# w2's first 352 rows on eight DMA engines instead of 224 on five, in a decode kernel of attention and a gated feed-forward

## The chip, the cores and the metric

The kernel runs on one core of a Trainium2 chip. Its time is the device time of one execution in microseconds; several executions are timed and the median is given. A profile belongs to one further execution, with its own time: there, "span" is the time from the first instruction's start to the last one's end on the core.

## What is computed

Two sequences, one new token each (B = 2), model width 512, 32 heads of 128, a cache of 4096 keys and values a head, all in bfloat16. An attention output and a small feed-forward output are mixed by a gate that each sequence computes from its own token:

```python
def _A_ref(x, k_cache, v_cache, wq, wo):
    q = (x @ wq)                                        # (2, 32, 1, 128)
    scores = jnp.einsum("bhqd,bhkd->bhqk", q, k) * (Dh ** -0.5)
    p = _softmax(scores, axis=-1)
    o = jnp.einsum("bhqk,bhkd->bhqd", p, v)
    return o.reshape(B, Sq, Hq * Dh) @ wo               # wo: 4096 x 512

def _B_ref(x, w1, w2):
    h = jnp.maximum(x @ w1, 0)                          # w1: 512 x 1376
    return h @ w2                                       # w2: 1376 x 512

g = _sigmoid((x * gate_w).sum(-1, keepdims=True))
return g * _A_ref(x, ...) + (1 - g) * _B_ref(x, ...)
```

The two caches are 134 MB of the 145 MB that are read. There is little arithmetic for each byte, so the kernel is a stream of loads with work fitted in between.

## The kernel before, in words

**Program order.** Every instruction is written down once for its engine by `P.add`, with the names of the events it waits for (`waits`), DMA semaphores with counts (`dwaits`) and the event it signals. `emit` (L67) writes these lists out, one for each of SP, TensorE (pe), VectorE (dve), ScalarE (act) and GpSimd (pool). An engine runs its own list in order; across engines only the events count.

**The load stream.** All large loads are issued by SP, in one list (L215 to L242). First w1 and wq, then sixteen units of 8 MB: eight of the K cache and eight of the V cache, in the order k0 to k4, v0, k5, v1, k6, v2, k7, v3 to v7. The units go round three regions of `kv`, 64 KB a partition each (`NREG`, `REG`); a unit's load waits until the unit three places earlier has been consumed (`freed`). The last V unit comes in two pieces, v7a (192 of 256 rows a partition) and v7b (64). Behind them, in the region of the fourteenth unit (v5), come the weights of the output stage, all issued when v5 has been consumed: w2p (L231 and L234), wo in three pieces wo0, wo1, wo2 (L236: 16, 12 and 4 rows a partition), and w2a, w2b, w2c, w2d (L239). The last SP issue is the store of the result (L242), which waits for both casts.

A load over 128 partitions moves eight rows on each of the sixteen DMA engines, and each engine works through its own rows of SP's list in order.

**How w2 is laid out.** w2 has 1376 rows of 512 numbers, 1 KB each. `W2` (L210) lists pieces as (semaphore, first row, rows a partition, first block). Before the change 1152 rows, nine blocks of 128, go over all 128 partitions: w2a and w2b with three consecutive rows a partition, w2c with two, w2d with one. The first 224 rows go over few partitions: 220 of them as eleven consecutive rows on 20 partitions, by four transfers of five partitions each (`j::4`, L231), 11 KB a partition, and four rows as one block on four partitions (L234). Together 21 blocks (`NF`).

**The feed-forward half.** `ffn_h` (L306) runs early: for each block four matmuls (L312) over w1 columns spaced by the block's rows a partition, so that h comes out with row i of a block on the partition where w2's row lies; then ScalarE writes relu(h) x (1 - g) into `hT` (L318), once for each sequence and each group of blocks with the same number of partitions.

**The end.** `v_unit` (L423) multiplies probabilities by V; `v_extract`, `v_gather` and `o_scale` bring the attention output together, `o_place` spreads it over the partitions as `oW`. The output stage adds matmuls of one block each, two halves of 256 columns (`step`, L475), into one accumulator: `project_first` (L479) the w2p blocks, of which five stand ahead of v7's gather and the others behind it, waiting for all five w2p transfers (count 80); then `project` (L485) the 32 blocks of wo and, in order, those of w2a, w2b, w2c and w2d, each group waiting for its own transfer. The block with `stop` lets VectorE and ScalarE cast the two halves (L496, L498), and SP stores 2 KB.

**TensorE's code.** TensorE has some 2180 of the program's 2394 recorded instructions; beside the loads, the DMA queue "instruction" (q8) brings 16 KB pieces of code while the kernel runs.

Of the kernel before, what the change touches and what calls it, by code (L numbers as in the profile page):

```python
# [84 lines left out]
def bass_gated_mix__gqa_block_cached__dense_activation_relu__decode_kernel(  # L85
# [16 lines left out]
    kv = sb("kv", [128, NREG, REG], bf16)  # L102
# [26 lines left out]
    hT = sb("hT", [128, 21, 2], bf16)  # L129
# [24 lines left out]
    def psf(p0, p1, c0, n):  # L154
        return PSF[p0:p1, c0:c0 + n]

    for e in ("pe", "dve", "act", "pool"):
        P.sems[e] = nc.alloc_semaphore(e + "_ev")
    names = ["x", "gw", "wq", "w1", "v7a", "v7b", "w2p", "wo0", "wo1", "wo2", "w2a", "w2b", "w2c", "w2d", "cast", "out"]
    sem = {n: nc.alloc_semaphore("sem_" + n) for n in names}  # L160
    sem_reg = [nc.alloc_semaphore(f"sem_reg{s}") for s in range(NREG)]

# [13 lines left out]
    def freed(what):  # L176
        kind, u = what
        return f"pe_sc_{u}" if kind == "k" else f"pe_v_{u}"

    def sp(fn, waits=(), dwaits=()):  # L180
        P.add("sp", fn, waits=waits, dwaits=dwaits)
# [4 lines left out]
    def dve(fn, waits=(), signal=None, dwaits=()):  # L186
        P.add("dve", fn, waits=waits, signal=signal, dwaits=dwaits)

    def act(fn, waits=(), signal=None, dwaits=()):
        P.add("act", fn, waits=waits, signal=signal, dwaits=dwaits)  # L190

    def pe(fn, waits=(), signal=None, dwaits=()):
        P.add("pe", fn, waits=waits, signal=signal, dwaits=dwaits)
# [10 lines left out]
    wo_reg = place[("v", 7)] + 1  # L204
    WO = wo_reg % NREG
    wo_sb = kv[:, WO, 0:16384]
    w2_sb = kv[:, WO, 16384:27136].rearrange("p (r n) -> p r n", n=512)


    W2 = (("w2p", 0, 11, 0), ("w2p", 220, 1, 11), ("w2a", 224, 3, 12), ("w2b", 608, 3, 15), ("w2c", 992, 2, 18), ("w2d", 1248, 1, 20))  # L210
    NF = 21

    act(lambda e: e.dma_start(x_sb[0:2], A_x.rearrange("b s d -> (b s) d")).then_inc(sem["x"], 16))
    act(lambda e: e.dma_start(x_sb[2:3], gate_w.rearrange("(o d) -> o d", o=1)).then_inc(sem["gw"], 16))
# [2 lines left out]
    for n, what in enumerate(order):  # L217
        if n >= NREG:
            waits = [freed(order[n - NREG])]
        else:  # L220
            waits = ["pe_h", "dve_setup", "act_q"] if n == C else []
# [5 lines left out]
        else:  # L227
            sp(lambda e, n=n, what=what: e.dma_start(kv[:, n % NREG, :], unit_in(what)).then_inc(sem_reg[n % NREG], 16),
               waits=waits)
    for j in range(4):  # L230
        sp(lambda e, j=j: e.dma_start(w2_sb[j:20:4, 0:11, :].rearrange("p r n -> p (r n)"),  # L231
                                      B_w2[0:220, :].rearrange("(p r) n -> p (r n)", r=11)[j::4]).then_inc(sem["w2p"], 16),
           waits=([freed(order[wo_reg - NREG])] if j == 0 else []))
    sp(lambda e: e.dma_start(w2_sb[0:4, 11, :], B_w2[220:224, :]).then_inc(sem["w2p"], 16))  # L234
    for i, (a, b) in enumerate(((0, 16), (16, 28), (28, 32))):
        sp(lambda e, i=i, a=a, b=b: e.dma_start(wo_sb[:, a * 512:b * 512], A_wo.rearrange("(p r) n -> p (r n)", r=32)[:, a * 512:b * 512])  # L236
           .then_inc(sem[f"wo{i}"], 16))
    for name, row, n, r0 in W2[2:]:
        sp(lambda e, name=name, row=row, n=n, r0=r0: e.dma_start(  # L239
            w2_sb[:, r0:r0 + n, :].rearrange("p r n -> p (r n)"),  # L240
            B_w2[row:row + 128 * n, :].rearrange("(p r) n -> p (r n)", p=128)).then_inc(sem[name], 16))
# [64 lines left out]
    def ffn_h():  # L306
        for ft in range(NF):
            row, n, r0 = [(row, n, r0) for _, row, n, r0 in W2 if r0 <= ft < r0 + n][0]
            m = 20 if ft < 11 else 4 if ft == 11 else 128
            for t in range(4):  # L310
                o = t * DFF + row + ft - r0
                pe(lambda e, ft=ft, t=t, o=o, n=n, m=m: e.matmul(psf(0, m, H_C0 + 2 * ft, 2), lhsT=w1_sb[:, o:o + (m - 1) * n + 1:n],  # L312
                                                            rhs=xT32[:, t, 0:2], start=(t == 0), stop=(t == 3)),
                   dwaits=([(sem["w1"], 16)] if ft == 0 and t == 0 else []),
                   signal=("pe_h" if ft == NF - 1 and t == 3 else None))
        for b in range(2):
            for p, r0, r1 in ((20, 0, 11), (4, 11, 12), (128, 12, NF)):
                act(lambda a, b=b, p=p, r0=r0, r1=r1: a.activation(  # L318
                    out=hT[0:p, r0:r1, b], in_=psf(0, p, H_C0 + 2 * r0, 2 * (r1 - r0))[:, b::2], func=ACT.Relu, scale=gm[0:p, b:b + 1]),
                    waits=(["pe_h", "act_gm"] if b + r0 == 0 else []), signal=(f"act_h{b}" if r1 == NF else None))  # L320

# [134 lines left out]
    def o_scale(b):  # L456
        dve(lambda v: v.tensor_reduce(out=Osum[:], in_=psf(0, 32, O_C0, 512).rearrange("p (c d) -> p d c", c=4), axis=AX.X, op=ALU.add),
            waits=[f"pe_g_{4 * b + 3}"], signal=f"dve_S{b}")
        dve(lambda v: v.tensor_scalar(out=O_sb[:, b, :], in0=Osum[:], scalar1=rinv[:, b:b + 1],
                                      scalar2=gb[0:32, b:b + 1], op0=ALU.mult, op1=ALU.mult),  # L460
            waits=[f"dve_S{b}"], signal=f"dve_O{b}")
# [11 lines left out]
    def step(w, m, start=False, stop=False, waits=[], dwaits=[]):  # L473
        for g in range(2):
            pe(lambda e, g=g: e.matmul(psf(64 * g, 64 * g + 2, FIN_C0, 256), lhsT=w, rhs=m[:, 256 * g:256 * g + 256],  # L475
                                       start=start, stop=stop, tile_position=(0, 64 * g), skip_group_check=True),
               waits=(waits if g == 0 else []), dwaits=(dwaits if g == 0 else []), signal=("pe_fin" if stop and g else None))

    def project_first(r0, r1):  # L479
        for r in range(r0, r1):  # L480
            k = 20 if r < 11 else 4
            step(hT[0:k, r, :], w2_sb[0:k, r, :], start=(r == 0), waits=(["act_h1", "act_exp1"] if r == 0 else []),
                 dwaits=([(sem["w2p"], 80)] if r == 0 else []))

    def project():  # L485
        lands = {0: "wo0", 16: "wo1", 28: "wo2"}
        for r in range(32):
            step(oW[:, r, :], wo_sb[:, r * 512:r * 512 + 512], waits=(["act_oW"] if r == 0 else []),
                 dwaits=([(sem[lands[r]], 16)] if r in lands else []))
        for name, _, n, r0 in W2[2:]:  # L490
            for r in range(r0, r0 + n):
                step(hT[:, r, :], w2_sb[:, r, :], stop=(r == NF - 1), dwaits=([(sem[name], 16)] if r == r0 else []))
        for g in range(2):
            src, dst = psf(64 * g, 64 * g + 2, FIN_C0, 256), out_sb[:, 256 * g:256 * g + 256]
            if g == 0:
                dve(lambda e, src=src, dst=dst: e.tensor_copy(out=dst, in_=src).then_inc(sem["cast"], 1), waits=["pe_fin"])  # L496
            else:
                act(lambda e, src=src, dst=dst: e.activation(out=dst, in_=src, func=ACT.Copy).then_inc(sem["cast"], 1), waits=["pe_fin"])  # L498
# [5 lines left out]
    w_block(0)  # L504
    w_block(1)
    ffn_h()
    for u in range(4):
        k_turn(u)
# [10 lines left out]
    for v in range(8):  # L519
        v_unit(v)  # L520
        if v == 3:
            o_denominator()
        v_extract(v)
        if v < 3:
            spread(v + 1)
            k_turn(5 + v)
            k_scores(5 + v)
            if v == 0:
                w_block(7)
        if v == 2:  # L530
            sm_max(1)
            sm_exp(1)
            sm_turn(1)
        if v == 7:
            project_first(0, 5)
        v_gather(v)
        if 3 <= v < 7:
            spread(v + 1)
        if v == 3:
            o_scale(0)  # L540
    project_first(5, 12)
    o_scale(1)
    o_place()
    project()
    tail_sp[0]()

# [31 lines left out]
```

## Time and profile before

| | |
|---|---|
| median of 3 runs | 343.61 us (343.56 to 343.7) |
| the profiled execution: its time, its span | 343.64 us, 342.3 us |
| bytes read | 145.43 MB, 425 GB/s over the span |
| TensorE / VectorE busy | 189.9 us / 155.2 us |
| w2p issued (first of four) | at 294.73 us |
| last block's matmuls begin | at 340.35 us |
| cast, store issued | 340.67 us, 341.11 us |

Each core has sixteen DMA engines; "DMA share" in a stretch is the mean busy share of the sixteen. The chain of waits follows the work that ended last back to what released it. A row of the timeline gives the start, the duration, the engine and line, the operation, the tile written and those read, and in brackets how long the engine had been idle and what ended that. "hT" as source marks w2's blocks, "oW" those of wo.

### The profile page before, as it was taken

To read this page: it belongs to the slowest core of one execution; us is meant where nothing else is said; L and a number is where in the kernel's file an instruction comes from. 1 tells how busy PE (TensorE), PEld (TensorE's weight loads), DVE (VectorE), ACT (ScalarE), POOL (GpSimd) and SP (SyncE) were. 2 spreads that over 40 slices of the span, in tenths; PEclk is the share of its full clock that TensorE was granted. 3 is DMA by queue.
4 is the path that set the end of the run, shared out by engine and by line. 5 is a ranking of instruction groups with operands and counts; after the bars stand their busy time and mean duration, and the time that the engine had idled before them with its cause. 6 is when DMAs were issued, how large, how long until landed. Compare 5 with 4: busy or idle time off the path is not lost.

```text
span 342.3 us, 2394 instructions
## 1 busy us (share of the span) xinstructions
PE 189.9 (55%) x1282; PEld 39.4 (12%) x898; DVE 155.2 (45%) x41; ACT 13.1 (4%) x31; POOL 43.1 (13%) x55
## 2 busy tenths in 40 slices
PE   0160069795968909850993059800994522506385
PEld 0040001010100101010011001200111201102132
DVE  1010797979899769219900694009925000000010
ACT  2010000000000020000000000000003000000000
POOL 2000000000000004042005000050003150413200
PEclk9995559899896967995799559965898585858589
DMA  8998989899998989899999999899999999999996
GB/s 349 429 484 375 483 375 483 383 475 414 438 490 368 490 383 475 383 469 391 467 406 446 429 429 483 375 484 406 452 406 452 406 446 421 437 440 427 389 422 253
DMA packets 3810, 145.56 MB, mean 425 GB/s; under 512 B 445, under 2 KB 582, under 8 KB 1094
## 3 DMA queue, kind: packets, MB, share of 16 engines
q1 hardware_dynamic: 3796, 145.43, 98.6%
q8 instruction: 8, 0.13, 0.2%
q10 hardware_dynamic: 6, 0.00, 0.0%
HBM read 145.43 MB, written 0.00 MB: 425 GB/s over the span
## 4 chain that ended last, share of the span: by engine, by line
DMA 64%; PE 23%; DVE 10%; SPq 2%; issue 0%
DMA kv<-in_A_k_cache_dram 43%; PE PS L340 14%; DMA kv<-in_B_w_dram 11%; DVE kv L335 10%; DMA kv<-in_A_v_cache_dram 10%; PE PS L368 5%; PE PS L423 3%; SPq L231 1%; SPq L239 0%; SPq L236 0%; PE PS L475 0%; PE PS L443 0%; SPq L234 0%; DVE ptm L496 0%; SPq L216 0%
## 5 line engine op out<-in xcount | busy, mean ns | idle before, releaser
L335 DVE STREAM_TRANSPOSE kv<-kv 128x8192 uint32<-128x8192 uint32 x16 | 138.5, 8690 | 80.3 <-DMA kv<-in_A_k_cache_dram 80.3
L340 PE MATMUL PS<-kv,zero 128*128 128x512 bf16 x384 | 117.5, 417 | 0.0
L368 PE MATMUL PS<-kv,zero 128*128 128x512 bf16 x128 | 54.1, 423 | 89.6 <-DVE kv L335 81.5
L423 PE MATMUL PS<-kv,ptm 128*32 128x512 bf16 x512 | 40.0, 459 | 33.8 <-DMA kv<-in_A_v_cache_dram 33.8
L368 PEld LDWEIGHTS PS<-kv,zero 128*128 128x128 bf16 x128 | 13.3, 104 | 203.6 <-issue 112.3
L406 POOL TENSOR_TENSOR ptm<-E,mask 128x512 bf16<-128x512 bf16 x32 | 32.2, 1039 | 10.9 <-DVE E L397 10.0
L434 DVE TENSOR_TENSOR X<-PS,maskc 128x512 f32<-128x512 f32 x1 | 0.7, 691 | 63.7 <-PE PS L423 63.7
L423 PEld LDWEIGHTS PS<-kv,ptm 128*32 128x32 bf16 x512 | 16.4, 112 | 58.4 <-issue 49.7
L438 POOL TENSOR_TENSOR X<-X,maskc 128x512 f32<-128x512 f32 x7 | 7.3, 1038 | 112.6 <-ACT X L437 112.6
L328 POOL TENSOR_TENSOR zero<-q_sb,mask 128x32 bf16<-128x32 bf16 x8 | 1.9, 251 | 151.2 <-PE PS L340 132.4
L443 PE MATMUL PS<-X,zero 128*32 128x512 f32 x16 | 8.5, 614 | 6.8 <-POOL X L438 6.6
L437 ACT ACTIVATE X<-PS 128x512 f32<-128x512 f32 x7 | 4.2, 596 | 142.4 <-PE PS L423 142.4
L292 PE MATMUL PS<-kv,zero 128*32 128x512 bf16 x32 | 3.6, 628 | 8.9 <-DMA kv<-in_A_wq_dram 8.9
L374 DVE TENSOR_REDUCE zero<-PS 128x2 f32<-128x2048 f32 x2 | 4.5, 2272 | 7.2 <-PE PS L340 7.2
L397 DVE STREAM_TRANSPOSE E<-E 128x2048 bf16<-128x2048 bf16 x2 | 4.6, 2311 | 4.7 <-ACT E L389 4.7
L299 DVE STREAM_TRANSPOSE ptm<-PS 128x1024 f32<-128x1024 f32 x1 | 1.2, 1249 | 11.9 <-PE PS L292 11.9
L381 ACT ACTIVATE nrow<-mmax 128x32 f32<-128x32 f32 x2 | 0.5, 228 | 138.0 <-DVE mmax L378 138.0
L475 PE MATMUL PS<-kv,oW 128*2 128x256 bf16 x64 | 3.8, 272 | 2.4 <-DMA kv<-in_A_wo_dram 2.4
L496 DVE CAST ptm<-PS 2x256 bf16<-2x256 f32 x1 | 0.4, 412 | 9.1 <-PE PS L475 9.1
L389 ACT ACTIVATE E<-PS,negm 128x1024 bf16<-128x1024 f32 x4 | 4.4, 1109 | 0.6 <-DVE negm L385 0.6
L270 PE MATMUL PS<-kv 3*128 3x3 bf16 x4 | 0.3, 167 | 6.5 <-DMA kv<-in_gate_w_dram 6.5
L475 PE MATMUL PS<-kv,hT 20*2 20x256 bf16 (+2 forms) x42 | 3.2, 269 | 0.9 <-DMA kv<-in_B_w_dram 0.8
(43 smaller groups left out, 26.5 us busy)
## 6 DMA issues: line engine op xcount, KB each, us to landing
kv<-in_A_v_cache_dram SPq DMA_DIRECT2D x1, 6144.0 KB, 47.5
kv<-in_A_wq_dram SPq DMA_DIRECT2D x1, 4096.0 KB, 14.9
kv<-in_A_v_cache_dram SPq DMA_DIRECT2D x1, 2048.0 KB, 52.0
kv<-in_A_wo_dram SPq DMA_DIRECT2D x1, 2048.0 KB, 34.3
kv<-in_A_wo_dram SPq DMA_DIRECT2D x1, 1536.0 KB, 37.6
kv<-in_B_w_dram SPq DMA_DIRECT2D x1, 1376.0 KB, 5.8
kv<-in_B_w_dram SPq DMA_DIRECT2D x2, 384.0 KB, 39.1
kv<-in_A_wo_dram SPq DMA_DIRECT2D x1, 512.0 KB, 38.4
```

What stands on the lines that cost most here:

```text
L335: dve(lambda v, h=h: v.transpose(out=reg[:, 8192 * h:8192 * (h + 1)], in_=reg[:, 8192 * h:8192 * (h + 1)]), dwaits=([landed(what)] if h == ...
L340: return e.add_instruction(mybir.InstMatmult(name=nc.get_next_instruction_name(), engine=mybir.EngineType.PE, ins=[e.lower_ap(rhs), e.lowe ...
L368: return e.matmul(dst, lhsT=w, rhs=m, start=first, stop=final, skip_group_check=True)
L374: dve(lambda v: v.tensor_reduce(out=mpad[:, 0:2], in_=PSF[:, 0:2048].rearrange("p (x h q) -> p h x q", h=2, q=16), axis=AX.XY, op=ALU.max) ...
L389: act(lambda a, h=h: a.activation(out=E[:].rearrange("p (x h q) -> p h x q", h=2, q=16)[:, h], in_=PSF[:, 0:2048].rearrange("p (x h q) -> ...
L397: dve(lambda v: v.transpose(out=E[:], in_=E[:]), waits=[f"act_exp{b}"], signal=f"dve_et{b}")
L406: pool(lambda g, src=src, dst=dst: g.tensor_tensor(out=dst, in0=src, in1=msk, op=ALU.mult), waits=(([f"dve_et{b}"] if ub == 0 else []) + ( ...
L423: pe(lambda e, ci=ci, t=t: e.matmul(psf(32 * t, 32 * t + 32, c0, 512), lhsT=ptm[:, ci].rearrange("p c h -> p (c h)"), rhs=rows[:, 512 * ci ...
L437: act(lambda e: e.activation(out=X2[:], in_=src, func=ACT.Copy), waits=[f"pe_v_{v}"], signal=f"act_x_{v}")
L438: pool(lambda e: e.tensor_tensor(out=X, in0=X, in1=msk, op=ALU.mult), waits=[f"act_x_{v}"] + ([] if v else ["dve_setup"]), signal=f"pool_x ...
L443: pe(lambda e: e.matmul(psf(0, 32, O_C0, 512), lhsT=selx[:, 24 - 8 * ub:56 - 8 * ub], rhs=X2[:], start=(ub == 0), stop=(ub == 3), skip_gro ...
L475: pe(lambda e, g=g: e.matmul(psf(64 * g, 64 * g + 2, FIN_C0, 256), lhsT=w, rhs=m[:, 256 * g:256 * g + 256], start=start, stop=stop, tile_p ...
```

## The change

The first 352 rows of w2 take the place of the 224: 32 partitions with eleven consecutive rows each, by four transfers of eight partitions; the transfer of four rows is gone. The other 1024 rows are eight blocks over 128 partitions, in transfers of five, two and one rows a partition instead of three, three, two and one. The blocks become 19, and the matmuls of `ffn_h`, the relu's groups and the steps of the output stage follow.

```diff
-    W2 = (("w2p", 0, 11, 0), ("w2p", 220, 1, 11), ("w2a", 224, 3, 12), ("w2b", 608, 3, 15), ("w2c", 992, 2, 18), ("w2d", 1248, 1, 20))
-    NF = 21
+    W2 = (("w2p", 0, 11, 0), ("w2a", 352, 5, 11), ("w2b", 992, 2, 16), ("w2c", 1248, 1, 18))
+    NF = 19
...
     for j in range(4):
-        sp(lambda e, j=j: e.dma_start(w2_sb[j:20:4, 0:11, :].rearrange("p r n -> p (r n)"),
-                                      B_w2[0:220, :].rearrange("(p r) n -> p (r n)", r=11)[j::4]).then_inc(sem["w2p"], 16),
+        sp(lambda e, j=j: e.dma_start(w2_sb[j:32:4, 0:11, :].rearrange("p r n -> p (r n)"),
+                                      B_w2[0:352, :].rearrange("(p r) n -> p (r n)", r=11)[j::4]).then_inc(sem["w2p"], 16),
            waits=([freed(order[wo_reg - NREG])] if j == 0 else []))
-    sp(lambda e: e.dma_start(w2_sb[0:4, 11, :], B_w2[220:224, :]).then_inc(sem["w2p"], 16))
...
-    for name, row, n, r0 in W2[2:]:
+    for name, row, n, r0 in W2[1:]:
...
-            m = 20 if ft < 11 else 4 if ft == 11 else 128
+            m = 32 if ft < 11 else 128
...
-            for p, r0, r1 in ((20, 0, 11), (4, 11, 12), (128, 12, NF)):
+            for p, r0, r1 in ((32, 0, 11), (128, 11, NF)):
...
-            k = 20 if r < 11 else 4
-            step(hT[0:k, r, :], w2_sb[0:k, r, :], start=(r == 0), waits=(["act_h1", "act_exp1"] if r == 0 else []),
-                 dwaits=([(sem["w2p"], 80)] if r == 0 else []))
+            step(hT[0:32, r, :], w2_sb[0:32, r, :], start=(r == 0), waits=(["act_h1", "act_exp1"] if r == 0 else []),
+                 dwaits=([(sem["w2p"], 64)] if r == 0 else []))
...
-    project_first(5, 12)
+    project_first(5, 11)
```

## The prediction

> **What bounds the kernel now.** I read the chain of waits first.
>
> ```profile
> DMA 64%; PE 23%; DVE 10%; SPq 2%; issue 0%
> DMA kv<-in_A_k_cache_dram 43%; PE PS L340 14%; DMA kv<-in_B_w_dram 11%; DVE kv L335 10%; DMA kv<-in_A_v_cache_dram 10%; PE PS L368 5%; PE PS L423 3%; SPq L231 1%; SPq L239 0%; SPq L236 0%; PE PS L475 0%; PE PS L443 0%; SPq L234 0%; DVE ptm L496 0%; SPq L216 0%
> ...
> q1 hardware_dynamic: 3796, 145.43, 98.6%
> q8 instruction: 8, 0.13, 0.2%
> ```
>
> The loads keep the sixteen DMA engines busy for 98.6% of the span, so TensorE's and VectorE's shares are work inside that stream: the end comes when the last weight bytes land. How the stream ends is in the timeline and in the table by stretches (us; PE, PEld, DVE, ACT, POOL; clock; DMA share; GB/s).
>
> ```profile
> 338.49 0.20 PEld L475 LDWEIGHTS PS<-kv,hT 128*2 128x2 bf16 x6 [0.65 <-DMA kv<-in_B_w_dram]
> ...
> 340.07 0.09 PEld L475 LDWEIGHTS PS<-kv,hT 128*2 128x2 bf16 x4 [0.43 <-DMA kv<-in_B_w_dram]
> 340.35 0.08 PEld L475 LDWEIGHTS PS<-kv,hT 128*2 128x2 bf16 x2 [0.20 <-DMA kv<-in_B_w_dram]
> ...
> 340.67 0.41 DVE L496 CAST ptm<-PS 2x256 bf16<-2x256 f32 x1 [9.05 <-PE PS L475]
> 341.11 0.27 SPq L242 DMA_DIRECT2D out_dram<-ptm  x1
> ```
>
> ```profile
> 337.00:337.50 0.50, 0.50 (x14) 0.34 (x8) 0.00 (x0) 0.00 (x0) 0.00 (x0) 1.00 1.01 389
> 337.50:338.00 0.50, 0.50 (x12) 0.28 (x8) 0.00 (x0) 0.00 (x0) 0.00 (x0) 1.00 0.99 377
> 338.00:338.50 0.50, 0.15 (x6) 0.01 (x2) 0.00 (x0) 0.00 (x0) 0.00 (x0) 1.00 0.82 322
> 338.50:339.00 0.50, 0.49 (x6) 0.17 (x6) 0.00 (x0) 0.00 (x0) 0.00 (x0) 1.00 0.84 322
> 339.00:339.50 0.50, 0.06 (x2) 0.07 (x4) 0.00 (x0) 0.00 (x0) 0.00 (x0) 1.00 0.70 252
> ```
>
> TensorE waits for w2a to w2d as each lands. From 338.0 the DMA share is 0.82 to 0.84: about three of sixteen engines have nothing left while the others carry on for 1.5 us.
>
> Which three? The trace holds every packet's start, duration and size, but no engine number. On one engine a packet starts within some 5 ns of the end of the one before, so packets can be strung into sixteen chains (span time: stamp less 11.40 us, the first instruction's). Near ties can swap two chains' names, but not a chain's load. They end in three groups:
>
> | chains | what they carry besides the even share | last packet ends, us |
> |---|---|---|
> | 5 | four 11,264 B packets of w2p (four of the five also a 1 KB row) | 339.65, .67, .67, .80, .83 |
> | 8 | one 16 KB instruction fetch (q8) each | 339.08 (the fetch at 331.5), 339.29 to 339.57 |
> | 3 | nothing | 337.69, 337.96, 338.06 |
>
> The eight fetches fell on eight different chains, none on the five. A fetch costs its chain 1.47 us: the first took 0.98 us and stretched the next 64 KB packet from 2.42 to 2.93. The four w2p packets cost 1.71 (a chain of the five goes from 325.13 to 326.84). The even share drains alike everywhere, so the last of the five sets the end: 339.83, 0.52 before TensorE's wait ends at 340.35.
>
> **The change part by part.**
>
> *Even share of w2.* Before, each engine moves 72 rows there: sixteen 3 KB packets (two groups of eight, 0.98 and 0.96 us, in a chain of the five), eight of 2 KB (0.65) and eight of 1 KB (0.35): 2.94 us. After, 64 rows: eight of 5 KB, 2 KB and 1 KB. No 5 KB packet is in the trace. Eight 4 KB packets take 1.27 us (about 157 ns each), eight of 12 KB 3.68 (460 ns). At 12 KB's rate per byte 5 KB is 192 ns, at 4 KB's 196, on the line between the two 195. I take 195: 1.56 us, together 2.56. Saved on every engine: 0.38 us (0.37 to 0.40).
>
> *The 4-row transfer goes.* 1 KB and its semaphore write: 0.05 us on four of the five.
>
> *w2p on eight engines.* The five keep their four packets; three more get four each, +1.71. If the three are the ones with nothing extra, the chains end at: four of the five, less 0.43, 339.24, .24, .37, .40; the fifth, less 0.38, 339.27; the three, plus 1.33, 339.02, .29, .39; the fetched, less 0.38, 338.70 to 339.19. The last is 339.40: **0.43 us earlier.** That the transfers nest is in the trace: all four five-row transfers used the same five chains, and the four-row one four of these. By the Trainium skill ("DMA: Bandwidth & Descriptors", "Why a DMA increments its semaphore by 16 and not by 1") a load from SP runs on as many engines as the largest number up to 16 that divides its slowest dimension, the lowest-numbered ones; five agrees with the trace, and for eight partitions it gives engines 0 to 7.
>
> No redistribution can do much more. The mean end of the sixteen chains is 339.21; the change takes 16 x 0.38 + 0.20 off and puts 3 x 1.71 on, net 1.15, or 0.07 each: 339.14. A perfect balance would gain 0.69.
>
> *Behind the last landing.* Still one block (two matmuls), the cast and the store: nothing. Ahead of it w2a now brings five blocks at once: ten matmuls at 0.06 us (32 wo matmuls in 1.91) are 0.60, and w2b lands about 0.65 later. Uncovered, at most 0.05 would show.
>
> *Wait for w2p (80 becomes 64).* TensorE reaches it at 328.62. The three new chains finish v7's rows by 325.24 at the latest and w2p by 326.95; with 0.52 to landing 327.5, covered by 1.1 us. Behind it stand project_first, v_gather, o_place and wo; a lag of a few tenths would be lost in the wait for wo1 (1.67 us at 336.23).
>
> *SP's queue.* Twelve issues become ten. Two of L239's are held up (13.3 us, then 6.6, to 320.8), yet no w2d packet could start before its chain reached it, 337.3 at the earliest, and the store L242 behind them waits 20.3 us anyway. Nothing on the path.
>
> *TensorE and ScalarE early.* ffn_h: 8 of 84 matmuls fewer (84 in 2.7 us, so 0.26 us) and two activations of 0.24. These release k2's load (L228, which waited 1.0 us for L312), but that load queues behind k0 and k1, and k0 lands at 36.8: hidden; uncovered it would be a gain of 0.26. Weights of 32 columns for 20: the 128-column ones take no longer (101 ns against 124). project_first: two matmuls fewer, under the same cover.
>
> *The fetches.* TensorE loses 24 of its 2180 instructions (12 matmuls with their weight loads), so each fetch comes 16 to 20 instructions later. The last, at 331.5, moves to about 333, still before its chain's end; it cost 1.08 us there and can cost 1.47, which ends that chain at 339.09. Nothing.
>
> **Sum:** -0.43 us (-0.36 to -0.50 with the 5 KB price, the 0.05 and chain readings of 0.03). The profiled execution took 343.64 us (span 342.3 and 1.3 around it), 0.03 above the median, so the median goes from 343.61 to **343.18**. Measurements of this kernel can tell about 0.2% (0.69 us) from no change; the forecast lies within it.
>
> **The rivals.**
>
> *A. The added engines are fetched ones (slower).* If one of the three carries a fetch, it ends at 339.29 to 339.57 plus 1.33, that is 340.6 to 340.9: 0.8 to 1.1 us after today's end, 344.4 to 344.7. It decides as soon as one of the three is among the seven earlier-fetched chains; if only the one fetched last (339.08), 340.41 and 344.2. TensorE's wait for w2p would end near 328.9, still under cover. For it: chains have no numbers, and the free three need not be the next three. Against it: eight fetches hit eight different engines and spared all five. Either fetches go round a fixed half of the engines (one half spares the five always) or round all sixteen from some start (four starts of sixteen spare them, one of these sparing the next three too). At even odds beforehand the first weighs 0.25 (half of 0.5), the second 0.125, of which a quarter is also good: 0.28 in 0.375, or three in four that the three are free.
>
> *B. No change.* If a full set of engines slowed each other, the three idle ones' work would only lengthen the rest: about 343.6. Against it: 3 KB packets take 121 to 133 ns (median 124) throughout, and share and rate fall together (1.01 and 389, then 0.82 and 322), so no engine speeds up when three are done.
>
> *C. One of the added engines is slow in itself.* The chains' mean 64 KB packets differ by 1.5 ns at most (2419.8 to 2421.3); the worst, over 120 packets, is 0.18 us late: 339.57, or 343.35. The Trainium skill ("DMA: Bandwidth & Descriptors", "Latency and other measured facts") says engines 7 and 15 are usually slower in traces; the means here show no such pair.
>
> *D. More than forecast.* Even the perfect balance ends at -0.69, 342.9; it needs a cheaper 5 KB packet or a fetch that no longer happens.
>
> **How the numbers follow.** Forecast 0.68 (own range 343.0 to 343.35), A 0.22 (0.19 of it at 344.4 to 344.7), B 0.04, C 0.03, D 0.03. Faster by over 0.2% is D alone, 0.03; slower by over 0.2% needs 344.3, A less its mild case, 0.19; the rest 0.78. Both signs hold much, so the range runs from 343.0 less what D leaves, 342.9, to A's 344.7.
>
> **What would show it.** In the packets: eight chains with four 11,264 B packets, eight with a fetch, none with both; 5 KB packets near 195 ns; all sixteen ending within 0.7 us; DMA share near 1 until about 338.7 in place of 0.82; the last wait at L475 ending near 339.9. A chain with both loads, ending near 340.7 with the share low before it, proves me wrong in favour of A. An earlier fetch start than 331.5 for the last, or a ninth, would upset the fetch step.

## The result, and the profile after

The changed kernel takes 344.69 us (median of 8, 344.38 to 345.69) against 343.63 (343.56 to 343.77): slower, by a ratio of 1.0036 with a 95% interval of 1.0026 to 1.0045. The forecast was 343.18; what came is rival A's case. Five of the eight executions took 344.38 to 344.80 and three 345.51 to 345.69.

The profiled execution took 344.58 us, its span is 343.3. The chain of waits and the queues' table of the changed kernel look as before:

```profile
DMA 65%; PE 22%; DVE 10%; SPq 1%; issue 0%
...
q1 hardware_dynamic: 3668, 145.43, 98.3%
q8 instruction: 8, 0.13, 0.1%
```

The same bytes and the same eight code fetches, but 0.3 points less of the span filled. Where the gap lies is in the table by stretches (columns as before: stretch, us, PE, PEld, DVE, ACT, POOL, granted clock, DMA share, GB/s):

```profile
337.50:338.00 0.50, 0.42 (x8) 0.35 (x10) 0.00 (x0) 0.00 (x0) 0.00 (x0) 1.00 1.01 401
338.00:338.50 0.50, 0.50 (x14) 0.40 (x10) 0.00 (x0) 0.00 (x0) 0.00 (x0) 1.00 0.83 328
338.50:339.00 0.50, 0.50 (x14) 0.34 (x10) 0.00 (x0) 0.00 (x0) 0.00 (x0) 1.00 0.91 352
339.00:339.50 0.50, 0.50 (x10) 0.18 (x4) 0.00 (x0) 0.00 (x0) 0.00 (x0) 1.00 0.57 205
339.50:340.00 0.50, 0.00 (x0) 0.00 (x0) 0.00 (x0) 0.00 (x0) 0.00 (x0) 1.00 0.12 47
340.00:340.50 0.50, 0.09 (x2) 0.09 (x4) 0.00 (x0) 0.00 (x0) 0.00 (x0) 1.00 0.13 47
340.50:341.00 0.50, 0.50 (x10) 0.26 (x6) 0.00 (x0) 0.00 (x0) 0.00 (x0) 1.00 0.04 14
```

The kernel before has 0.14 in its last stretch with loads; there five chains end within the stretch, at 339.65 to 339.83:

```profile
339.50:340.00 0.50, 0.43 (x6) 0.11 (x6) 0.00 (x0) 0.00 (x0) 0.00 (x0) 1.00 0.14 47
```

A share of 0.12 to 0.13 is two engines of sixteen (0.125). In the changed kernel two engines work alone from 339.5 to 340.5, and TensorE has next to nothing to do. Its timeline ends so:

```profile
329.08 0.71 PE L474 MATMUL PS<-kv,hT 32*2 32x256 bf16 x10 [0.45 <-DMA kv<-in_B_w_dram]
...
333.97 3.31 PE L474 MATMUL PS<-kv,oW 128*2 128x256 bf16 x32 [1.78 <-DMA kv<-in_A_wo_dram]
...
337.58 1.91 PE L474 MATMUL PS<-kv,oW 128*2 128x256 bf16 x32 [0.30 <-DMA kv<-in_A_wo_dram]
340.41 0.42 PEld L474 LDWEIGHTS PS<-kv,hT 128*2 128x2 bf16 x10 [1.21 <-DMA kv<-in_B_w_dram]
...
341.02 0.09 PEld L474 LDWEIGHTS PS<-kv,hT 128*2 128x2 bf16 x4 [0.19 <-DMA kv<-in_B_w_dram]
341.32 0.08 PEld L474 LDWEIGHTS PS<-kv,hT 128*2 128x2 bf16 x2 [0.22 <-DMA kv<-in_B_w_dram]
...
341.64 0.41 DVE L494 CAST ptm<-PS 2x256 bf16<-2x256 f32 x1 [9.79 <-PE PS L474]
```

The last wait ends at 341.32 instead of 340.35: 0.97 us, which is the whole difference of the two profiled executions (344.58 less 343.64 is 0.94).

Strung into chains as in the prediction, the packets say which two engines:

| chains of the changed kernel | what they carry besides the even share | last packet ends, us |
|---|---|---|
| 6 | four w2p packets | 339.10 to 339.45 |
| 2 | four w2p packets and a code fetch (at 150.9 and at 184.7) | 340.80, 340.54 |
| 6 | a code fetch | 339.19 to 339.48 |
| 2 | nothing | 337.83, 338.00 |

Without the two, the last chain would have ended at 339.48, 0.35 us before the kernel of before. 340.80 and 0.52 for the landing is 341.32, where the last wait ends.

### The profile page after: what moved, and what is told of

Same layout as the page of the kernel before. It is cut to its first block, busy times and chain, and to the rows that moved or that the text cites. A ratio compares the mean times of both kernels' runs of the same rounds, so it can differ in the third digit from the quotient of the medians.

```text
span 343.3 us, 2366 instructions
## 1 busy us (share of the span) xinstructions
PE 187.6 (55%) x1270; PEld 40.7 (12%) x886; DVE 155.4 (45%) x41; ACT 12.8 (4%) x29; POOL 43.1 (13%) x55
## 4 chain that ended last, share of the span: by engine, by line
DMA 65%; PE 22%; DVE 10%; SPq 1%; issue 0%
DMA kv<-in_A_k_cache_dram 44%; PE PS L339 14%; DMA kv<-in_B_w_dram 12%; DVE kv L334 10%; DMA kv<-in_A_v_cache_dram 10%; PE PS L367 5%; PE PS L422 3%; SPq L231 1%; SPq L235 0%; PE PS L474 0%; PE PS L442 0%; DVE ptm L494 0%; SPq L216 0%; SPq L215 0%
## 5 line engine op out<-in xcount | busy, mean ns | idle before, releaser
L339 PE MATMUL PS<-kv,zero 128*128 128x512 bf16 x384 | 113.8, 406 | 0.0
L367 PE MATMUL PS<-kv,zero 128*128 128x512 bf16 x128 | 52.5, 410 | 94.4 <-DVE kv L334 85.1
L474 PE MATMUL PS<-kv,oW 128*2 128x256 bf16 x64 | 5.2, 332 | 2.1 <-DMA kv<-in_A_wo_dram 2.1
L311 PEld LDWEIGHTS PS<-zero,kv 128*32 128x32 bf16 (+1 forms) x76 | 3.9, 138 | 0.4 <-issue 0.4
```

The costliest lines, as they stand in the source:

```text
L339: return e.add_instruction(mybir.InstMatmult(name=nc.get_next_instruction_name(), engine=mybir.EngineType.PE, ins=[e.lower_ap(rhs), e.lowe ...
L367: return e.matmul(dst, lhsT=w, rhs=m, start=first, stop=final, skip_group_check=True)
```

## The experiments

**Theory:** the added engines 5 to 7 are partly engines that also fetch TensorE's code, and such an engine ends last. **Rivals:** the fetches lie on 8 to 15 and the eight engines, or the groups of five, cost time in themselves; later also: TensorE's half clock in the output stage.

### Numbering the engines with 16-byte loads: mark5, mark8, mark8b

```diff
         if what == ("v", 7):
+            for j in range(1, 16):
+                sp(lambda e, j=j: e.dma_start(scr[0:j, j - 1, :], B_w2[0:j, 0:8]).then_inc(sem["mark"], 16))
```

> The kernel before, with fifteen loads of 1 to 15 rows of 16 bytes ahead of v7a; if a load of j rows runs on the j lowest engines, engine i carries 15 - i of these small packets, which gives every chain of packets its engine's number. Theory: the five w2p chains are engines 0 to 4, the eight code fetches lie on eight of engines 5 to 15, and at least one of 5, 6, 7 is among them. Rival: the fetches lie on 8 to 15, the three free chains are 5, 6, 7, and what lengthens the changed kernel is something else. Time 343.6 to 344.6 (the small packets put up to 0.5 us on engine 0).

> The changed kernel with the same fifteen small loads. Theory: one to three of engines 5, 6, 7 carry both the four 11,264 B packets and a code fetch and end 0.8 to 1.1 us after the rest; time 344.4 to 346. Rival: no engine carries both, and the last chain is late for another reason (5 KB packets well over 0.2 us, or packets that wait).

> The same kernel once more. If the eight engines of the fetches are the same in every execution, the same numbers as in the run before; if the start moves from one execution to the next, other numbers, still none of 0 to 4, and that would explain why the changed kernel's times spread over 1.3 us and those of before over 0.2.

Measured: 345.59, 345.82 and 345.71 us. These runs settled nothing about the numbers: packets 6 ns apart on engines that run within some 10 ns of each other could not be told apart. They were also not small in effect: v7b's rows on four of the five w2p chains end at 326.6 to 326.7 in mark5 against 325.1 to 325.3 before, 1.5 us more for 15 or fewer packets of 9 ns each, and as many semaphore writes. Nor is the engine idle meanwhile: data and semaphore writes alternate in steps of some 6 ns, but of the sixteen 48 KB packets of v7a that come first behind them, eleven took 1.9 to 3.7 us, where those of the kernel before took 1.82. Why, these runs do not show.

### Numbering them with 768-byte loads: id5, id8

```diff
+    for j in range(2, 16):
+        sp(lambda e, j=j: e.dma_start(kv[0:j, WO, 27136 + 384 * (j - 2):27136 + 384 * (j - 1)], B_w2[0:j, 0:384]).then_inc(sem["mark"], 16))
     for i, (a, b) in enumerate(((0, 16), (16, 28), (28, 32))):
```

> The kernel before with fourteen loads of 2 to 15 rows of 768 bytes between w2p and wo, so that a chain's number of 768 B packets tells its engine (14 on engines 0 and 1, 15 - i on engine i). Theory: the five w2p chains have 14, 14, 13, 12 and 11 of them, the fetches lie on eight of engines 5 to 15, one or more of 5, 6, 7 among them. Rival: the fetches lie on 8 to 15 here and move when the program changes. Time up to 0.6 us over that of before, 343.6 to 344.3.

> The changed kernel with the same fourteen loads. Theory: the two or three chains that end last have 8 to 10 of the 768 B packets (engines 5 to 7), four 11,264 B packets and a fetch; the free chains have 7 or fewer. Rival: other chains end last. Time 344.4 to 346.

Measured: 346.04 and 346.08 us (against 343.66 and 344.69 the small loads cost 2.4 and 1.4 us, not 0.6). Now the chains that run apart from the crowd can be read. On one engine the packets follow each other in steps of 0.039 us, and engine i, from 1 up, carries 15 - i of them. In id8 the last of them, on engines that had both a fetch and w2p to do first, start at (us):

```
328.457 .496 .535 .574 .613 .652 .690 .729 .768                    9 packets
328.628 .667 .706 .744 .783 .822 .861 .900 .939 .977               10 packets
```

Nine and ten packets are engines 6 and 5. The first ones, on engines that had neither, form series of seven and five: engines 8 and 10 (from 325.288 and 325.157), and one chain has none, engine 15. In id5, where only engines 0 to 4 carry w2p, the early series have eight, seven and five: engines 7, 8 and 10, and again 15 has none. Both executions had seven fetches by then, and 5, 6 and the other five of 8 to 15, that is 9 and 11 to 14, are the seven late ones. The eighth, at 332.3 and 333.0, fell on the chain with five in id8, engine 10. So the eight fetches lie on **5, 6, 9, 10, 11, 12, 13 and 14**; 0 to 4, 7, 8 and 15 fetch nothing. Of the three engines that the change adds, two fetch. The series of 14 down to 0 also rest on a load of j rows using engines 0 to j - 1, as the Trainium skill has it ("DMA: Bandwidth & Descriptors", "Why a DMA increments its semaphore by 16 and not by 1"); the trace agrees, with eight chains that carry w2p in the changed kernel and five before.

### Other executions of the changed kernel: after_b, after_c, after_d

No edit.

> The changed kernel once more, for another execution's packets. From the chains numbered so far (fetches on engines 5, 6, 9, 10, 11, 12, 13 and 14, one after the other, from a start that moves): two w2p chains carry a fetch, whichever in order, none of the three others does, and the time is 344.4 to 344.8. An execution of 345.5 to 345.7 would show two fetches on one w2p chain, or a late one that costs more than 1.5 us. Rival: the fetches fall on any of engines 5 to 15, so that none, one or three w2p chains carry one.

> The same kernel as the run before it, another execution: again two w2p chains with a fetch and 344.4 to 344.8, or, at 345.5 to 345.7, two fetches on one w2p chain or a late one that costs more than 1.5 us.

> The same kernel a third time: again two w2p chains with a fetch and 344.4 to 344.8, or, at 345.5 to 345.7, two fetches on one w2p chain or a late one that costs more than 1.5 us.

Measured: 345.69, 344.48 and 344.52 us. In all three, as in the first profile, exactly two of the eight w2p chains carry a fetch and end last: 340.83 and 340.99, 340.63 and 340.70, 340.68 and 340.72. In the first profile it was the third and the fourth fetch, in these the fifth and the sixth (near 243 and 274): which of the fetches they are differs between executions, their number does not. That fits eight fetches that go once round eight engines from a start that moves.

The expectation for 345.69 was wrong: after_b's last chain ends only 0.2 to 0.3 us later than the others', with one fetch on each of the two chains. Its extra 1.2 us lies in TensorE, at the granted clock of the last stretches of after_b:

```profile
339.00:339.50 0.50, 0.50 (x8) 0.33 (x6) 0.00 (x0) 0.00 (x0) 0.00 (x0) 0.50 0.52 191
340.00:340.50 0.50, 0.50 (x9) 0.26 (x5) 0.00 (x0) 0.00 (x0) 0.00 (x0) 0.50 0.13 51
341.00:341.50 0.50, 0.50 (x8) 0.32 (x6) 0.00 (x0) 0.00 (x0) 0.00 (x0) 0.50 0.00 0
341.50:342.00 0.50, 0.50 (x10) 0.27 (x6) 0.00 (x0) 0.00 (x0) 0.00 (x0) 0.50 0.00 0
```

and its timeline:

```profile
337.77 3.07 PEld L474 LDWEIGHTS PS<-kv,oW 128*2 128x2 bf16 x32 [1.69 <-DMA kv<-in_A_wo_dram]
...
340.93 1.47 PEld L474 LDWEIGHTS PS<-kv,hT 128*2 128x2 bf16 x16
...
342.73 0.41 DVE L494 CAST ptm<-PS 2x256 bf16<-2x256 f32 x1 [10.64 <-PE PS L474]
```

At a clock of 0.50 the 32 matmuls behind wo1 take 3.16 us (337.77 to 340.93), against 1.9 at full clock before, and w2's sixteen follow without a wait: the loads are done at 341.0 and TensorE ends 1.7 us later. In after_c the clock was 1.00 again from about 339, and TensorE waited for data as usual.

That is a second bound, and it stands in the kernel before too. There wo1's matmuls start earlier:

```profile
336.23 1.91 PE L475 MATMUL PS<-kv,oW 128*2 128x256 bf16 x32 [1.67 <-DMA kv<-in_A_wo_dram]
```

At after_b's 0.099 us a matmul (3.16 for 32), the 50 matmuls from there on would end near 341.2 and the kernel take some 344.2 (an estimate). Eight of the 64 timed executions of the kernel before took 344.0 to 344.4; none of these was profiled, so whether half clock is their cause is open. In the changed kernel the bound lies higher, because a transfer lands when its last engine is done: wo1's last packet ends at 336.99 instead of 335.63 in the two first profiles, and its matmuls start at 337.4 to 337.8 in the four executions.

### Fewer engines added: seven

```diff
-    W2 = (("w2p", 0, 11, 0), ("w2p", 220, 1, 11), ("w2a", 224, 3, 12), ("w2b", 608, 3, 15), ("w2c", 992, 2, 18), ("w2d", 1248, 1, 20))
+    W2 = (("w2p", 0, 8, 0), ("w2a", 224, 3, 8), ("w2b", 608, 3, 11), ("w2c", 992, 2, 14), ("w2d", 1248, 1, 16))
...
-        sp(lambda e, j=j: e.dma_start(w2_sb[j:20:4, 0:11, :].rearrange("p r n -> p (r n)"),
+        sp(lambda e, j=j: e.dma_start(w2_sb[j:28:4, 0:8, :].rearrange("p r n -> p (r n)"),
...
```

> The kernel before with its 224 rows of w2p on seven engines instead of five: 28 partitions with eight rows each, by four transfers of seven, no transfer of four rows; the groups of w2 as before. Each of engines 0 to 6 gets four 8 KB packets (about 1.26 us on the line from 4 to 12 KB) instead of 1.71 on five. Theory (5 and 6 fetch code, 0 to 4 do not): 0 to 4 end 0.45 us earlier than before, but 5 and 6 end at 340.55 to 340.8, 0.7 to 1.0 us after the last chain of before: 344.3 to 344.6. If the fetches were not there, or on 8 to 15 only: the fetched chains' 339.56 is last, 343.35.

Measured: 344.57 us (344.48 to 345.13), ratio 1.0026 (1.0014 to 1.0039). Five w2p chains end at 339.18 to 339.37, the two with a fetch at 340.49 and 340.66, the fetched ones without w2p at 339.54 to 339.76. The same bytes as before, no larger groups, a quarter less on each engine (32 KB for 44), and still 0.9 us slower: it is the place of the packets that costs.

### Fewer fetches: lite5, lite8, lite8_b, lite8_c

```diff
-        for rp in range(4):
+        for rp in (0, 2):
...
-            for blk in range(4):
+            for blk in (0,):
...
-        for ci in range(64):
+        for ci in (0, 1, 2, 3, 48, 60, 61, 62, 63):
...
```

> The kernel before with most of TensorE's attention work left out (an eighth of the score matmuls and nine of the 64 value matmuls of a unit), so that TensorE has some 740 instructions for 2180 and two or three code fetches for eight. Theory: the end is still set by the five w2p chains, which carry no fetch: 343.4 to 343.7. Rival (TensorE's own work sets the end): a microsecond or more faster.

> The changed kernel with the same work left out. Theory: with two or three fetches the chance is small that one falls on engines 5 to 7 (in the changed kernel's profile the third and fourth did), the eight w2p chains end at about 339.4 and the kernel is faster than the one before: 343.1 to 343.35, so 0.3 to 0.5 us below the five-engine kernel with the same work left out. If the eight engines or the groups of five rows cost time in themselves, it stays 0.6 us or more slower than that one.

> The eight-engine kernel with most of TensorE's attention work left out, another execution. Its ten times fell into 343.2 to 343.65 and 344.57 to 344.73; the profile at 343.2 had no fetch on a w2p chain. Theory: an execution near 344.6 shows one or both early fetches on a w2p chain, which ends near 340.7; one near 343.4 shows none. Rival: both have none, and the slower ones have TensorE at half clock in the output stage.

> The same kernel as the run before it, another execution: near 344.6 with a fetch on a w2p chain that ends near 340.7, or near 343.4 with none; by the rival the slower ones have no such chain and a half clock at the end.

Measured: lite5 343.75 us (343.61 to 343.93), ratio 0.9999 (0.9990 to 1.0009); lite8 344.11 (343.2 to 344.73), ratio 1.0010 (0.9997 to 1.0023); lite8_b 343.34, lite8_c 343.52. Leaving out most of TensorE's attention work changed the five-engine kernel's time by nothing: its end is a matter of loads. lite8's ten times fall into 343.20 to 343.65 and 344.57 to 344.73, five each. The three profiles, all of the lower group, have three fetches, two early and one near 338. None is on a w2p chain, and the w2p chains end at 338.9 to 339.6. This is the forecast's picture: in lite8's profile the last wait ends at 339.94, where the forecast had it near 339.9, and that execution took 343.20. The lower group lies 0.1 to 0.55 us below lite5's median; three of its seven times lie in the forecast's own range, 343.0 to 343.35. If the fetches go round the eight engines from a start that moves, two early ones fall on 5 or 6 for three starts of eight, and the third does for one more. The upper group was never profiled, so that it carries such a fetch is inferred. Half clock alone does not explain it. In lite8_c the clock was 0.50 until beyond 338, TensorE's own work ended last, and the time was 343.52. At 0.50 to the end, the 80 matmuls from 333.2 or 333.4 on would make 344.1 to 344.3 (an estimate from after_b's rate), below the upper group. In lite8 both groups have executions with the same mean clock of 0.776, and lite5, with the same work left out, has no such group.

### The groups of w2 alone: five621, five621_b

```diff
-... ("w2a", 224, 3, 12), ("w2b", 608, 3, 15), ("w2c", 992, 2, 18), ("w2d", 1248, 1, 20))
+... ("w2a", 224, 6, 12), ("w2b", 992, 2, 18), ("w2c", 1248, 1, 20))
```

> The kernel before with only the groups of w2 changed, to six, two and one rows a partition (no change of engines). All theories: sixteen 3 KB packets (1.94 us on a chain) become eight of 6 KB (about 1.86 by the line from 4 to 12 KB), one issue fewer: 0.0 to 0.15 us faster than before, 343.45 to 343.65. If larger groups in themselves cost time, slower by up to 0.5.

> Five engines with w2's groups of six, two and one rows again, in more rounds, as the version that could beat both kernels: the last chain ended 0.16 us before that of the kernel before, so 343.4 to 343.55 against 343.6 to 343.7, a ratio of 0.9993 to 0.9998; without that gain 1.000.

Measured: 343.46 us (343.31 to 343.66), ratio 0.9994 (0.9984 to 1.0003), and 343.52 (343.42 to 343.73), ratio 0.9997 (0.9988 to 1.0006). The last w2p chain ends at 339.67 and 339.72 (before: 339.83). Larger groups cost nothing; a gain of 0.1 to 0.2 us is what the packets show, and the intervals do not exclude none. Of the versions that compute everything it is the only one below both kernels, by less than can be claimed.

## Why the prediction was wrong

**The step that failed** is in "w2p on eight engines": "If the three are the ones with nothing extra". They are not. The three chains with nothing are engines 7, 8 and 15; the three added are 5, 6 and 7, and 5 and 6 fetch code. So the last chain ended at 340.80 in the first profile, not at 339.40. The odds behind it, three in four, came from two arrangements only, one of two halves of the engines or a run of eight neighbours. The set measured, 5, 6 and 9 to 14, is neither. The first profile alone was compatible with any eight of the eleven engines that carry no w2p; without an assumed arrangement all three of 5 to 7 are free in 1 of 165 cases.

**Rival A** named the place and the price: one engine with both loads ends at 340.6 to 340.9 and the kernel at 344.4 to 344.7. Measured: 340.54 to 340.99 in four profiles, and 344.69. There are two such engines, which costs what one does, as the last one sets the end. Part of the agreement is luck: the median also holds the three executions above 345.5.

**The sum for everything else held.** Engines 0 to 4 and 7 were to end at 339.02 to 339.40 and ended at 339.10 to 339.45; a fetch was priced at 1.47 us, and the two chains with both loads end 1.3 and 1.6 us after the mean of the w2p chains without one (339.23). The 5 KB packets, priced at 195 ns, took 199 or 200 ns (median of each profile), 0.04 us on a chain. The SP queue, the shorter feed-forward and the missing row moved nothing that can be seen. One reading was wrong without effect: the last fetch before, at 331.5, was put at 1.08 us, but the 12 KB packet behind it took 0.95 us for 0.46, so it cost some 1.56. Rival A's mild case, 344.2, rests on that reading. w2p did make TensorE wait, 0.45 us at 329.08 in the first profile, as rival A said, and the wait for wo0 that follows (1.78 us before 333.97) took it up.

**Rival B** falls with lite8's lower group, **C** with the numbers: engine 7, free of fetches, is among six w2p chains that end within 0.35 us.

**What no step had:** that TensorE's half clock can set the end. The stage was read at the clock of one profile, 1.00 from 334 to the last matmul. At 0.50 the matmuls behind wo1 take longer than the rest of the loads, and after_b shows the 1.2 us that this adds. The changed kernel's executions at 345.5 and 345.6 fit that, but were not profiled.

## What to carry to other kernels

When a load-bound kernel ends, string the packets into engines and ask what else each of them carries; an idle share of 3/16 says that there is room, not that the next three engines have it. Here a load over five, seven or eight partitions was a load on as many engines, always the same ones, so number the engines with such loads of different widths before work is moved there. And judge a stage that TensorE nearly fills at its half clock too.

## What the runs showed of the hardware

- TensorE's code came in 16,384 B packets, one engine each, eight in a run on the eight engines 5, 6 and 9 to 14, none on 0 to 4, 7, 8 or 15 in the executions numbered (id5, id8). With TensorE's instructions down from 2180 to some 740 there were three (lite5). One held its engine up by 1.4 to 1.6 us: 0.9 to 1.1 us for itself and about 0.5 us more in the load's packet behind it (before, after). The Trainium skill ("Runtime: NRT & Kernel Launch", "Terms") says that instruction memory is refilled in 16 KiB blocks; the packets agree.
- Fifteen loads of 16 B a row ahead of a large one cost the kernel 2 us (mark5, 345.59 against 343.63; 1.1 us in mark8, 345.82 against 344.69), though their packets last 9 ns: the first 48 KB packets behind them took up to 3.7 us instead of 1.82.
- The granted clock went between 0.50 and 1.00 near the end at times that differ from execution to execution: 1.00 from 328 to 340 in the kernel before, 0.50 from 336 to 342 in after_b. The 32 matmuls behind wo1 took 1.9 us in the one and 3.2 in the other.
